# Holding the attention's operand splits behind the tanh and the gate of their slot, in a one-core attention and SwiGLU chain

## The chip, the cores and the metric

The kernel runs on one core of a Trainium2 chip. The metric is the device time of one launch in microseconds. Three runs of the kernel before gave 1437.30, 1439.62 and 1440.31 us; the median, 1439.62 us, is the time before.

## The reference, cut to what matters

All arrays are fp32; batch 8, 8 heads, 576 rows, head size 64, 32 packing rows per head.

```python
def sm_attn(qq, kk, vv):                     # softmax(scale * qq @ kk.T) @ vv
    ...
p_packed = sm_attn(p, k, v)                  # 32 rows per head
x = sm_attn(q, p_packed, p_packed)           # 576 rows per head
x = x.transpose(0, 2, 1, 3).reshape(4608, 512)
h = x @ w_in                                 # 512 -> 2048
x = (h * sigmoid(h)) @ w_out                 # 2048 -> 512
out = (((x @ w1) * (x @ w2)) @ w3) @ w_out2  # 512 -> 1024 -> 512
```

## The kernel before

Nearly every product is made from split operands: an fp32 array is turned into a high part in fp32r (a copy, on ScalarE, L82) and a low part, the rest (a subtraction, on VectorE or GpSimd, L91), and TensorE does three matmuls, high by high, low by high and high by low (`mm3`, L98 to L100). A **split** below is this pair of operations.

The long first stage makes x from the attention and takes it through `w_in`, SiLU and `w_out`. It never makes x itself: the packed rows of a head are multiplied into `w_in` once (`PackIn`, "pack w_in": matmuls ps_m, results ms stored to m_d), and the softmax weights `a` of the second attention go through that product. The stage is a list of 256 **slots** (`items`): a slot is a batch b, one of two halves f of 288 tokens, and one of 16 column blocks m. In each slot, in the order of the code:

- `fetch` (from L782) brings a block of the product (mr) and splits it into mq, the high part on VectorE (L86), the low part on GpSimd;
- `emit_h`: six matmuls ps_h<-a,mq;
- `emit_x2`: twelve matmuls ps_x<-gh,wo for the slot three before (`LAG` = 3);
- `emit_g`: the **tanh** sg on ScalarE (L841), the **gate** gg = (sg + 1) * ps_h on VectorE (L846), then gg's split, gh on ScalarE and gl on GpSimd. ps_h has two banks, so the matmuls of a slot wait for the gate of the slot two before;
- steps of three **streams**: "x", the attention units `Pack` (first attention of one batch and half of its heads) and `Spread` (second attention), "y", `PackIn`, and "z", decoding of later weights. `over(lo, hi, units)` and `pack_in` spread a unit's steps evenly over slots lo to hi, and `due` counts the steps due by a slot: n * (i + 1 - lo) / (hi - lo), rounded up. That is a **place**.

While a unit's steps run, `HOOKS` prepare the next unit's operands: `load_v`, `turn0` and `turn1` (k or q rows in kq, split into x: high part on ScalarE, low part on VectorE, `Rows.turn`), `prepare` (the packing rows pr, split into pb, same engines), `split_v0` and, in the first step of a `Pack`, `split_v(1)` (the values vr, split into v in two parts: ScalarE, GpSimd). `PackIn.load_w` loads a piece of `w_in` (wz) and splits it into wi (ScalarE, GpSimd); three are loaded ahead (`WI` = 3) before the first ps_m. Units of the first two batches work unsplit (`plain`), so the splits start with batch 2.

Slots that the prediction speaks of: the steps of `Spread(1, 0)` and `Spread(1, 1)` lie in slots 5 to 13, the last two of them in slots 11 and 12, and hang the splits for `Pack(2, 0)` on these (x in slots 11 and 12, pb and the first part of v in 12). `Pack(2, 0)` to `Pack(3, 1)` have 16 steps over slots 26 to 37: two steps are due in slot 26 (second part of v, then `turn0` for the next unit), the third in slot 27 (`turn1`, `prepare`), the fourth in slot 28. The `PackIn` of batches 2 and 3 starts in slot 44, the next ones in slots 102 and 166.

What is written is not the order of issue. The program is given to a scheduler at build time (last lines of `kernel`: `schedule_with_timeline_sim=True`), which plays it through with estimated times and sets each engine's own order; an engine then takes its instructions strictly in that order, waiting on semaphores. An operation whose data are there early may be put ahead of a tanh that was written long before it. `tc.issue_after(ins)`, used by `hold`, forbids that: what a block issues on the engine of `ins` is put behind `ins` in that engine's order. It adds no waiting for data. `behind["sg"]` and `behind["gg"]` are the latest tanh and gate that the code has written. The kernel before uses `hold` for the later weights' work only (`decode_late`, `prepare_second`), and similar blocks for the late half of `fetch` and for transfers.

Of the kernel before, what the change touches and what calls it, by code (L numbers as in the profile page):

```python
# [23 lines left out]
def attention_swiglu_chain(  # L24
# [54 lines left out]
    V, A, T, G, DMA = nc.vector, nc.scalar, nc.tensor, nc.gpsimd, nc.sync  # L79

    def act_copy(dst, src, mul=1.0):
        A.activation(out=dst, in_=src, func=ACTF.Copy, scale=mul)  # L82

    def split_hi(hi, src, on_vector=False):
        if on_vector:
            V.tensor_copy(out=hi, in_=src)  # L86
        else:
            act_copy(hi, src)

    def split_lo(lo, src, hi, eng=None):  # L90
        (eng or V).tensor_tensor(out=lo, in0=src, in1=hi.bitcast(F32), op=ALU.subtract)  # L91

    def split(hi, lo, src, on_vector=False, eng=None):
        split_hi(hi, src, on_vector)
        split_lo(lo, src, hi, eng)
# [8 lines left out]
    def hold(*names):  # L104

        stack = ExitStack()
        for x in names:
            stack.enter_context(tc.issue_after(behind[x]))
        return stack

    def move(out, in_, eng=DMA):

        out, in_ = (x.bitcast(F32) if x.dtype == F32R else x for x in (out, in_))
        with tc.issue_after(behind[eng]) if eng in behind else ExitStack():
            return eng.dma_start(out=out, in_=in_)  # L115
# [184 lines left out]
    class Rows:  # L300
# [25 lines left out]
        def turn(self, f):  # L326

            if f not in self.halves or self.lane.plain:
                return
            if f == self.halves[0]:  # L330
                self.xp = self.lane.parts([128, 2, S], "x")
            x = [t[:, :, f * HS:(f + 1) * HS] for t in self.xp]
            split(*x, self.rows[f])
            self.x[f] = [[t[:, e] for t in x] for e in range(2)]

        def turn0(self):
# [22 lines left out]
    class Pack(Rows):  # L359
# [22 lines left out]
        def prepare(self):  # L382
            if not self.lane.plain:
                self.pb = self.lane.parts([128, 2, 128], "pb")
                split(*self.pb, self.p)

        v_in_pieces = False

# [15 lines left out]
        def split_v(self, f):  # L404
            if self.lane.plain:
                return
            if f == 0:
                self.vp = self.lane.parts([128, 5, 4, 64], "v")
            r, cs = self.PARTS[f]
            hi, lo, src = (x[0:r, cs] for x in (*self.vp, self.v))  # L410
            split_hi(hi, src)
            split_lo(lo, src, hi, G)

        def split_v0(self):
            self.vp = [self.v]
# [81 lines left out]
    class PackIn:  # L497
# [14 lines left out]
        def load_w(self, i):  # L512
            if i < 4 * CD:
                g, c = divmod(i, CD)
                z = at.tile([128, 512], F32, tag="z", name="wz", bufs=NZ)
                move(out=z, in_=wi_d[g, 128 * c:128 * c + 128])
                t = at.tile([128, 2, 512], F32R, tag="wi", name="wi", bufs=WI)
                split_hi(t[:, 0], z)
                split_lo(t[:, 1], z, t[:, 0], G)
                self.w[i] = t  # L520

        def steps(self):
# [427 lines left out]
    def prepare_second():  # L950

        attn.close()
        with tc.tile_pool(name="dec2", bufs=1, side="right") as dp:
# [73 lines left out]
            for n in range(2 * KM2 + 2):  # L1027
                with hold("sg", "gg", "h"):
                    if n > 1:
                        product(n - 2)  # L1030
                    if n < 2 * KM2:
                        turn(n)
                for y in range(2):
                    with hold("sg", "gg"):
                        if used[0] < min(len(late) - KM2, KM2 + 3 + 3 * (n + y) // 2):
                            step()
                        some(2)
                    yield
# [362 lines left out]
```

## Time and profile before

| | |
|---|---|
| median of three runs | 1439.62 us |
| the profiled execution's own time | 1437.96 us |
| its span on the core | 1436.1 us |
| PE (TensorE matmul) busy | 1390.7 us, 97% |
| PEld (TensorE weight load) busy | 1308.4 us, 91% |
| DVE (VectorE) busy | 901.6 us, 63% |
| ACT (ScalarE) busy | 672.2 us, 47% |
| POOL (GpSimd) busy | 605.5 us, 42% |
| mean granted clock of TensorE | 0.992 |

Times inside the execution are microseconds from the start of the span. The 256 tanhs run from 52 us to about 855 us; from there on only the second half of the chain runs. A row of a timeline gives start, duration, engine, line, operation, what is written and read, shape and count, and in brackets how long the engine stood idle before it and what ended that. A granted clock of 1.00 is 2.4 GHz, of 0.50 is 1.2 GHz. PE is busy nearly all the time, so what matters are the few microseconds in which it stands idle or runs at the lower clock.

### The profile page before, as it was taken

How to read it: one execution, taken by the hardware profiler on the slowest of the kernel's cores; microseconds unless marked ns; L12 is line 12 of the kernel's file. 1: busy time of each engine (PE TensorE's matmuls, PEld its weight loads, DVE VectorE, ACT ScalarE, POOL GpSimd, SP SyncE). 2: the span in 40 equal slices, each digit the busy share in tenths (PEclk: the TensorE clock that was granted, in tenths of full speed). 3: DMA queues.
4: the chain of work that ended last, by engine and by line, in shares of the span. 5: the costliest groups of instructions: out<-in, count | busy, mean ns of one | idle time of the engine just before them, and what ended most of it. 6: DMA issues, size and time to landing. Idle time of an engine off the chain costs nothing.

```text
span 1436.1 us, 25890 instructions
## 1 busy us (share of the span) xinstructions
PE 1390.7 (97%) x9548; PEld 1308.4 (91%) x9548; DVE 901.6 (63%) x1687; ACT 672.2 (47%) x1474; POOL 605.5 (42%) x626
## 2 busy tenths in 40 slices
PE   7799899999999999999999999999999999999998
PEld 5578899899999999999998998999999999999998
DVE  5897756558766488666578855635454553645453
ACT  6866556655666555664556544323232231322221
POOL 2778755856779657687567534100000000000000
PEclk9999899999999999999999999999999999999999
DMA  8697544844568343563557667011010110101000
GB/s 319 198 308 253 163 150 142 265 152 146 170 184 249 123 155 121 170 190 116 178 162 252 204 228 298 23 38 46 15 60 1 60 29 31 59 2 60 1 30 30
DMA packets 135967, 193.07 MB, mean 134 GB/s; under 512 B 14496, under 2 KB 92576, under 8 KB 135328
## 3 DMA queue, kind: packets, MB, share of 16 engines
q1 hardware_dynamic: 125344, 178.82, 39.1%
q10 hardware_dynamic: 10496, 12.59, 2.5%
q8 instruction: 75, 1.23, 0.4%
q14 instruction: 52, 0.43, 0.1%
HBM read 132.38 MB, written 58.98 MB: 133 GB/s over the span
## 4 chain that ended last, share of the span: by engine, by line
PE 70%; DVE 9%; DMA 7%; issue 4%; POOL 4%; ACT 4%; SPq 2%; ACTq 0%; DVEq 0%; POOLq 0%
PE ps_ab L1236 24%; PE ps_x L100 6%; PE ps_x L98 6%; PE ps_x L99 6%; PE ps_o L98 5%; PE ps_o L99 5%; PE ps_o L100 5%; PE ps_h L98 3%; PE ps_h L100 3%; PE ps_h L99 3%; SPq L115 2%; DMA mr<-m_d 1%; DMA m_d<-ms 1%; POOL z L189 1%; DVE sbd L251 1%
## 5 line engine op out<-in xcount | busy, mean ns | idle before, releaser
L98 PE MATMUL ps_x<-gh,wo 128*128 128x288 f32 x1024 | 301.9, 298 | 2.7 <-ACT gh L82 1.2
L99 PE MATMUL ps_x<-gh,wo 128*128 128x288 f32 x1024 | 301.0, 296 | 0.0
L100 PE MATMUL ps_x<-gl,wo 128*128 128x288 f32 x1024 | 289.1, 297 | 1.9 <-POOL gl L91 1.6
L91 POOL TENSOR_TENSOR gl<-gg,gh 128x288 fp32r<-128x288 f32 x256 | 227.9, 893 | 101.5 <-ACT gh L82 82.5
L1236 PE MATMUL ps_ab<-xct,w 128*128 128x256 f32 x1728 | 223.0, 284 | 1.7 <-DVE r L1257 1.4
L1236 PEld LDWEIGHTS ps_ab<-xct,w 128*128 128x128 f32 x1728 | 215.6, 190 | 3.0 <-DVE r L1257 1.6
L98 PEld LDWEIGHTS ps_x<-gh,wo 128*128 128x128 f32 x1024 | 193.0, 189 | 6.1 <-DVE xs L883 2.0
L99 PEld LDWEIGHTS ps_x<-gh,wo 128*128 128x128 f32 x1024 | 193.2, 189 | 2.1 <-issue 1.2
L100 PEld LDWEIGHTS ps_x<-gl,wo 128*128 128x128 f32 x1024 | 188.1, 189 | 4.3 <-POOL gl L91 3.6
L82 ACT ACTIVATE gh<-gg 128x288 fp32r<-128x288 f32 x256 | 112.8, 443 | 165.8 <-DVE gg L846 158.2
L91 POOL TENSOR_TENSOR mq<-mr,mq 128x256 fp32r<-128x256 f32 x168 | 136.7, 814 | 109.0 <-DVE mq L86 54.4
L846 DVE SCALAR_TENSOR_TENSOR gg<-sg,ps_h 128x288 f32<-128x288 f32 x256 | 114.6, 448 | 107.3 <-ACT sg L841 55.3
L1236 PE MATMUL ps_ab<-xcb,w 128*128 128x256 f32 x1296 | 177.5, 283 | 0.7 <-ACT w L82 0.4
L98 PE MATMUL ps_h<-a,mq 128*128 128x288 f32 x512 | 155.9, 305 | 18.0 <-DVE gg L846 13.8
L1236 PEld LDWEIGHTS ps_ab<-xcb,w 128*128 128x128 f32 x1296 | 168.1, 189 | 5.6 <-ACT w L82 0.6
L1257 DVE TENSOR_TENSOR r<-p,ps_ab 128x512 f32<-128x512 f32 x72 | 49.2, 683 | 184.3 <-PE ps_ab L1236 184.1
L99 PE MATMUL ps_h<-a,mq 128*128 128x288 f32 x512 | 152.4, 298 | 0.0
L100 PE MATMUL ps_h<-a,mq 128*128 128x288 f32 x512 | 151.9, 297 | 0.0
L841 ACT ACTIVATE sg<-ps_h 128x288 f32<-128x288 f32 x256 | 103.4, 404 | 82.3 <-PE ps_h L100 48.6
L98 PEld LDWEIGHTS ps_h<-a,mq 128*128 128x128 f32 x512 | 96.7, 189 | 25.9 <-DVE gg L846 19.0
L82 ACT ACTIVATE p<-ps_ab 128x512 f32<-128x512 f32 x72 | 43.1, 598 | 146.2 <-PE ps_ab L1236 139.8
L100 PE MATMUL ps_o<-w,abh 128*128 128x512 f32 x280 | 109.5, 391 | 0.0
(172 smaller groups left out, 2645.3 us busy)
## 6 DMA issues: line engine op xcount, KB each, us to landing
mr<-m_d SPq DMA_DIRECT2D x144, 128.0 KB, 2.6
raw<-in_moe_w_dram SPq DMA_DIRECT2D x32, 512.0 KB, 4.4
wz<-wi_d SPq DMA_DIRECT2D x48, 256.0 KB, 3.8
m_d<-ms SPq DMA_DIRECT2D x96, 128.0 KB, 3.0
x_d<-xs SPq DMA_DIRECT2D x20, 576.0 KB, 3.4
raw<-in_moe_w_out_dram SPq DMA_DIRECT2D x22, 512.0 KB, 4.3
out_dram<-ob SPq DMA_DIRECT2D x36, 256.0 KB, 2.0
vr<-in_v_dram SPq DMA_DIRECT2D x14, 640.0 KB, 4.1
```

Of the source, the lines that this page charges most:

```text
L82: A.activation(out=dst, in_=src, func=ACTF.Copy, scale=mul)
L91: (eng or V).tensor_tensor(out=lo, in0=src, in1=hi.bitcast(F32), op=ALU.subtract)
L98: T.matmul(out=dst, lhsT=wh, rhs=xh, start=start, stop=False)
L99: T.matmul(out=dst, lhsT=wl, rhs=xh, start=False, stop=False)
L100: return T.matmul(out=dst, lhsT=wh, rhs=xl, start=False, stop=stop)
L115: return eng.dma_start(out=out, in_=in_)
L189: G.tensor_tensor(out=z, in0=z, in1=word(I32, 0), op=ALU.add)
L251: (act_copy if plain else V.tensor_copy)(dst[r, 0, :, r], src[r])
L841: ins = A.activation(out=sg, in_=ps, func=ACTF.Tanh, scale=0.5)
L846: ins = V.scalar_tensor_tensor(out=gg, in0=sg, scalar=1.0, in1=ps, op0=ALU.add, op1=ALU.mult)
L1236: T.matmul(out=bank[:, x], lhsT=w[:, wp], rhs=xt[:, kt, xp], start=first and (x, kt, n) == (0, 0, 0), stop=last and (x, kt, n) == (1, 1, 2 ...
L1257: V.tensor_tensor(out=dst, in0=p, in1=q, op=op)
```

## The change

Four places get a `hold`: the splits of x and pb go behind the latest tanh on ScalarE and behind the latest gate on VectorE; the splits of v and wi go behind the latest tanh on ScalarE (their low parts run on GpSimd, to which no hold applies, but they need the high part first). Nothing is added, removed or resized, and the slots at which the code writes these operations are the same.

```diff
@@ -330,7 +330,8 @@   (Rows.turn)
             x = [t[:, :, f * HS:(f + 1) * HS] for t in self.xp]
-            split(*x, self.rows[f])
+            with hold("sg", "gg"):
+                split(*x, self.rows[f])
             self.x[f] = [[t[:, e] for t in x] for e in range(2)]
@@ -382,7 +383,8 @@   (Pack.prepare)
                 self.pb = self.lane.parts([128, 2, 128], "pb")
-                split(*self.pb, self.p)
+                with hold("sg", "gg"):
+                    split(*self.pb, self.p)
@@ -408,8 +410,9 @@   (Pack.split_v)
             hi, lo, src = (x[0:r, cs] for x in (*self.vp, self.v))
-            split_hi(hi, src)
-            split_lo(lo, src, hi, G)
+            with hold("sg"):
+                split_hi(hi, src)
+                split_lo(lo, src, hi, G)
@@ -515,8 +518,9 @@   (PackIn.load_w)
                 t = at.tile([128, 2, 512], F32R, tag="wi", name="wi", bufs=WI)
-                split_hi(t[:, 0], z)
-                split_lo(t[:, 1], z, t[:, 0], G)
+                with hold("sg"):
+                    split_hi(t[:, 0], z)
+                    split_lo(t[:, 1], z, t[:, 0], G)
                 self.w[i] = t
```

## Rows read from the trace of the kernel before

**Rows 1.** PE's waits from 100 to 700 us: total, times, longest

```profile
PE ps_h L98 <- DVE gg L846: 9.3, 12, 2.7
PE ps_s L98 <- DVE mbd L492: 1.9, 4, 0.8
```

**Rows 2.** Timeline of ACT, 145 to 147 us: the x splits and a tanh

```profile
145.45 1.26 ACT L82 ACTIVATE x<-kq 128x576 fp32r<-128x576 f32 x2
...
146.91 0.41 ACT L841 ACTIVATE sg<-ps_h 128x288 f32<-128x288 f32 x1
```

**Rows 3.** The tanh's line from 0 to 146.9 us: count, shortest/median/longest ns, first and last start

```profile
L841 ACT ACTIVATE sg<-ps_h x27: 383/396/415, 52.4 to 142.4; 128x288 f32<-128x288 f32 x27
```

**Rows 4.** Timeline of DVE, 149 to 154 us

```profile
149.09 1.27 DVE L91 TENSOR_TENSOR x<-kq,x 128x576 fp32r<-128x576 f32 x1
150.29 1.49 DVE L91 TENSOR_TENSOR pb<-pr,pb 128x256 fp32r<-128x256 f32 x1
151.70 0.44 DVE L846 SCALAR_TENSOR_TENSOR gg<-sg,ps_h 128x288 f32<-128x288 f32 x1
...
153.46 0.45 DVE L846 SCALAR_TENSOR_TENSOR gg<-sg,ps_h 128x288 f32<-128x288 f32 x1
```

**Rows 5.** Timeline of PE, 150 to 170 us, two matmuls after idle time

```profile
152.20 0.40 PE L98 MATMUL ps_h<-a,mq 128*128 128x288 f32 x1 [1.32 <-DVE gg L846]
...
168.55 0.61 PE L98 MATMUL ps_h<-a,mq 128*128 128x288 f32 x1 [2.69 <-DVE gg L846]
```

**Rows 6.** Timeline of POOL, 153 to 169 us

```profile
153.91 2.58 POOL L91 TENSOR_TENSOR wi<-wz,wi 128x512 fp32r<-128x512 f32 x2
...
159.96 1.34 POOL L91 TENSOR_TENSOR wi<-wz,wi 128x512 fp32r<-128x512 f32 x1
...
164.17 3.07 POOL L91 TENSOR_TENSOR v<-vr,v 128x768 fp32r<-128x768 f32 x2
```

**Rows 7.** Timeline of DVE, 161 to 169 us: the casts ahead of a gate

```profile
162.96 4.33 DVE L251 CAST sbd<-pkT 32x64 fp32r<-32x64 f32 x4
```

**Rows 8.** Instructions on tile sbd, whole span: count, shortest/median/longest ns, first and last start

```profile
L251 DVE CAST sbd<-pkT x48: 175/306/2066, 163.0 to 588.4; 32x64 fp32r<-32x64 f32 x48
```

**Rows 9.** Stretches: length, busy time of each engine, granted clock, DMA share, GB/s

```profile
82.00:95.00 13.00, 13.00 (x84) 11.47 (x83) 11.54 (x18) 9.62 (x22) 10.85 (x11) 1.00 0.92 283
95.00:111.00 16.00, 12.90 (x78) 10.31 (x78) 15.76 (x24) 8.94 (x18) 10.03 (x11) 1.00 0.93 306
141.00:153.00 12.00, 8.78 (x59) 7.46 (x58) 11.97 (x18) 8.15 (x20) 11.30 (x10) 1.00 0.57 172
153.00:164.00 11.00, 10.82 (x71) 10.59 (x71) 5.50 (x16) 7.35 (x18) 10.78 (x12) 0.84 0.73 209
164.00:176.00 12.00, 9.31 (x50) 9.08 (x49) 10.17 (x22) 3.61 (x9) 7.04 (x9) 0.72 0.24 73
200.00:215.00 15.00, 15.00 (x118) 15.00 (x117) 8.96 (x28) 7.33 (x18) 10.25 (x12) 1.00 0.56 177
```

**Rows 10.** Timeline of DVE, 83 to 104 us

```profile
83.78 1.54 DVE L91 TENSOR_TENSOR pb<-pr,pb 128x256 fp32r<-128x256 f32 x1
...
102.75 0.75 DVE L91 TENSOR_TENSOR x<-kq,x 128x576 fp32r<-128x576 f32 x1
103.42 0.44 DVE L846 SCALAR_TENSOR_TENSOR gg<-sg,ps_h 128x288 f32<-128x288 f32 x1
```

**Rows 11.** Instructions on tile pb, whole span: columns as in rows 8

```profile
L91 DVE TENSOR_TENSOR pb<-pr,pb x12: 408/412/1536, 83.8 to 549.6; 128x256 fp32r<-128x256 f32 x12
```

**Rows 12.** Timeline of POOL, 98 to 106 us: its longest idle time there

```profile
104.14 0.74 POOL L91 TENSOR_TENSOR mq<-mr,mq 128x256 fp32r<-128x256 f32 x1 [2.60 <-DVE mq L86]
```

**Rows 13.** Instructions on tile wi, whole span: the first matmul of each product

```profile
L98 PE MATMUL ps_m<-wi,mbd x48: 388/393/500, 236.6 to 647.0; 128*128 128x512 f32 x48
```

**Rows 14.** Timeline of DVE, 277 to 283 us

```profile
279.99 1.18 DVE L86 CAST mq<-mr 128x256 fp32r<-128x256 f32 x1 [3.33 <-DMA mr<-m_d]
```

**Rows 15.** Timeline of PE, 277 to 283 us

```profile
281.59 0.40 PE L98 MATMUL ps_h<-a,mq 128*128 128x288 f32 x1 [1.04 <-DVE gg L846]
```

## The prediction

> **What bounds the kernel now.** I read the stretches first, then PE's waits, then the timelines around the longest waits. From 200 us on PE is busy without a break for long stretches [rows 9], so only its idle time and its time at the lower clock can be won. In the 600 us in which the moved splits lie, PE waits 9.3 us in 12 places for a gate and 1.9 us in 4 for the blocks mbd [rows 1]. A gate is late when VectorE has other work queued ahead of it: from 95 to 111 us VectorE works 15.76 of 16 us, from 141 to 153 us 11.97 of 12, and there PE stands idle 16 - 12.90 = 3.1 and 12 - 8.78 = 3.2 us [rows 9]. After the second of these the granted clock falls: 0.84 over 11 us is 11 * 0.16 / 0.5 = 3.5 us at 1.2 GHz, and 0.72 over 12 us is 6.7 us; at half the rate these cost half their length, 1.75 and 3.35 us [rows 9].
>
> **What the change moves.** A hold only matters where a split now stands ahead of the tanh or gate of its slot. I paired the n-th split of a kind on ScalarE with the n-th that the plan of places issues, and counted tanhs. Of 132 splits 39 stand ahead: 12 of x, 8 of pb, 10 of v, 9 of wi. Most x and pb are early by one to nine slots, the second parts of v by 19 to 32, the first three wi of each of the three products by 15 to 45. The other 93 are behind already, some by five slots, and stay. An example: 27 tanhs have run by 146.9 us [rows 3], so the one at 146.91 is slot 27's, and the two x splits just before it [rows 2] are those of slots 26 and 27. Consumers are far: the first three wi run at about 152 us and their first matmul at 236.6 [rows 6, 13].
>
> **Slots 26 to 28.** On VectorE gate 27 starts at 151.70, behind x of slot 27 and pb, 1.27 and 1.49 us [rows 4]. Held, these follow it: it starts at 149.09 and ends at 149.5. They then end by 152.3 at the same lengths, before gate 28's 153.46, so gate 28 need not be later. PE's idle of 1.32 us before 152.20 [rows 5] goes: **-1.3 us** (0 to -1.3).
>
> **The clock after it.** With 3.2 - 1.3 = 1.9 us of idle in 12, the stretch is below the 3.1 in 16 from 95 to 111 us that kept the full clock [rows 9]. I count the first fall as gone: **-1.75 us**. The second I leave; the bounds are 0 and -1.75 - 3.35 = -5.1.
>
> **Slots 28 to 33.** The three wi of slot 44 take 2.58 + 1.34 = 3.9 us of GpSimd ahead of two v splits that run from 164.17, 3.07 us [rows 6]. Beside these v the four sbd casts take 4.33 us [rows 7], against a median of 0.31 each, 1.2 for four [rows 8], and they stand ahead of the gate for which PE waits 2.69 us [rows 5]. With the wi gone to slot 44 the v can run up to 3.9 us sooner, mostly before the casts. The v are in their own slots and stay in the order. I take **-2.0 us** of the wait; bounds 0 and -2.69.
>
> The Trainium skill (SBUF — State Buffer, Who interferes with whom) says that VectorE and GpSimd share one port pair under an exclusive lock, and that the loser is blocked for the whole instruction. These rows agree, a cast's longest being 2.07 us against 0.31. By that rule the casts would lose all of 4.33 - 1.2 = 3.1 us and the wait would go whole; the sum below would be 0.7 us lower. The same rule speaks against every GpSimd half that lands beside a VectorE chain in its new slot.
>
> **Slots 11 to 13.** Here the change brings work in. pb and both v now run around 83 us, in a stretch in which PE never idles (13.00 of 13), so nothing is won there [rows 9, 10]. pb and the first v go to slot 12, the stretch from 95 us whose VectorE is full. x of slot 12 stands ahead of gate 12 (102.75, then 103.42) [rows 10]; behind it, it delays gate 13 instead, which cancels. pb is new work ahead of gate 13: 0.41 us undisturbed, 1.54 beside GpSimd [rows 11, 10]. The v on GpSimd has a gap of 2.60 us [rows 12], and using it puts GpSimd beside pb, so I take the price beside it: **+1.5 us** (0.4 to 1.5).
>
> **v's second part in slot 26.** GpSimd is full from 141 to 153 us, 11.30 of 12 [rows 9]; half of a pair of v parts is 3.07 / 2 = 1.5 us [rows 6]. It pushes gl, which has three slots until its matmuls. **+0.4 us** (0 to 1.5), near nothing since PE's long waits are for gates and not for gl [rows 1].
>
> **Slots 66 to 68.** The wi of slot 102 run from 278 us. A cast of mq takes 1.18 us there and PE idles 1.04 us behind the gate after it; but the cast itself waited 3.33 us for a transfer, which stays [rows 14, 15]. **-0.7 us** (0 to -1.04).
>
> **Slots 85, 86, 149, 150.** v of these slots runs two or three slots early and ahead of the copies pk, whose chain pkT, sbd, mbd ends in the waits for mbd, 1.9 us in all [rows 1]. Held, pk goes first, but v then falls beside the same chain. **-0.8 us** (-1.9 to +1.4).
>
> **The rest** costs nothing as long as its cover holds. From 200 to 215 us PE is busy 15.00 of 15 us and GpSimd 10.25, which leaves room for the 3.9 us of wi [rows 9]; the first ps_m is 30 us away [rows 13]. The groups of slots 59, 72, 102, 122, 136 and 166 are alike; if GpSimd lacks the room, gl is late next. Bounds 0 to +1.5. No transfer is held, and none is issued earlier: a held split frees its source tile later, but the tiles are reloaded a unit later.
>
> **Sum.** -1.3 - 1.75 - 2.0 + 1.5 + 0.4 - 0.7 - 0.8 = -4.65 us. The profiled execution took 1437.96 us, 1.66 below the median of 1439.62, so 1433.3 there and **1435.0 us** as a median. The best ends give -1.3 - 5.1 - 2.69 + 0.4 - 1.04 - 1.9 = -11.6, the worst +1.5 + 1.5 + 1.4 + 1.5 = +5.9.
>
> **Rivals.**
>
> *Given back.* VectorE has the same work, and where it is full a split that is passed by one gate delays the next. For it: VectorE's 11.97 of 12 us, with decoding work queued there too [rows 9]. Against it: the 5.50 of 11 us right behind, where held work could go [rows 9]. Then the gate's 1.3 us, both falls of the clock and the waits of slots 85 and 149 stay, GpSimd's relief remains: -2.0 + 1.5 + 0.4 - 0.7 = -0.8, 1438.8 us, no change that a measurement shows.
>
> *Little is moved.* The scheduler's estimated times are not the chip's, and it may fill the freed places on VectorE with other work written earlier (decoding). Then the gates are as late as now and the time is about 1439.6. For it: decoding shares VectorE where it is full [rows 9]. Against it: gate 27 has no decoding between the splits and itself [rows 4].
>
> *Slower.* VectorE's chain in slots 11 to 15 becomes the bound. x of slot 12 and pb come between gates 12 and 13 with v on GpSimd beside them, and run at 1.27 and 1.54 instead of 0.75 and 0.41 us [rows 4, 10, 11]: +0.5 for x, +1.5 for pb as the sum has it. PE's idle of 3.1 us in that stretch becomes over 5, and the granted clock falls there as it does after 153 us, +1.75 for the shorter fall. With slots 26 to 33 given back (v's second part takes the room of the wi there, +1.5), this is 0.5 + 1.5 + 1.75 + 1.5 = +5.25 less 1.5 from the later slots (0.7 + 0.8), +3.75: 1443.4 us. It decides when PE idles over 5 us between 95 and 111 us.
>
> **How the numbers follow.** A measurement of this kernel tells about 0.2%, 2.9 us, from no change. My forecast has 0.47, all of it counted as faster; given back 0.22 and little moved 0.11, both within 0.2%; slower 0.20. The range reaches from the forecast with the second fall and the whole of the long wait gone too (-4.65 - 3.35 - 0.7 = -8.7, 1430.9, a little lower for the other bounds: 1430) up to the slower case, 1443.5. Cases of one sign do not hold most of it; the forecast's own range is 1430 to 1437.
>
> **What would show it.** Right: gate 27 directly behind its tanh, the wait of 2.69 us under 1 us, a granted clock near 1.00 from 153 to 164 us, three wi behind the 45th tanh. PE's waits for gates from 100 to 700 us near 5 us. Wrong: the same waits a slot or two later, a granted clock below 1.00 between 95 and 115 us, or new waits of PE for gl or for ps_m's operands.

## The result and the profile after

The kernel after takes **1451.43 us** (four runs, 1449.99 to 1453.49), the kernel before 1438.97 beside it: ratio 1.0092, 95% interval 1.0077 to 1.0106. It is slower by about 12.5 us, where 1435.0 was forecast. The hold does what it says: of the 132 splits none stands ahead of its slot's tanh or gate any more (39 did). So the rival "little is moved" is out; the work moved, and it cost.

The page's busy times after (engine, busy us, share of the span, instructions):

```profile
span 1451.3 us, 25880 instructions
PE 1395.6 (96%) x9548; PEld 1311.6 (90%) x9548; DVE 917.8 (63%) x1687; ACT 672.4 (46%) x1474; POOL 618.0 (43%) x626
```

VectorE is busy 16.2 us and GpSimd 12.5 us longer than before, with the same instructions: they stand in each other's way more. The tile x shows it, VectorE's 48 low parts of x before and after (count, shortest/median/longest ns, first and last start):

```profile
L91 DVE TENSOR_TENSOR x<-kq,x x48: 709/749/1869, 101.3 to 665.7; 128x576 fp32r<-128x576 f32 x48
L91 DVE TENSOR_TENSOR x<-kq,x x48: 740/912/3911, 105.9 to 689.8; 128x576 fp32r<-128x576 f32 x48
```

PE's waits of the kernel after from 100 to 700 us, to be set against [rows 1]:

```profile
PE ps_h L98 <- DVE gg L850: 14.5, 14, 4.3
PE ps_s L98 <- DVE mbd L495: 5.8, 4, 2.0
```

Gates cost 5.2 us more (9.3 before), mbd 3.9 more (1.9 before). The stretches of after, columns as in [rows 9]; the last line is that of 215 to 230 us before:

```profile
95.00:111.00 16.00, 13.28 (x86) 11.35 (x85) 15.96 (x25) 10.61 (x22) 10.55 (x10) 1.00 1.01 330
141.00:153.00 12.00, 9.69 (x67) 8.76 (x66) 12.00 (x16) 9.73 (x22) 11.37 (x10) 1.00 0.65 195
153.00:164.00 11.00, 6.32 (x39) 5.83 (x38) 10.08 (x15) 4.15 (x13) 10.07 (x11) 0.79 0.45 125
164.00:176.00 12.00, 12.00 (x87) 12.00 (x86) 6.31 (x12) 4.25 (x11) 7.13 (x8) 0.91 0.44 132
200.00:215.00 15.00, 15.00 (x118) 15.00 (x117) 8.11 (x24) 10.44 (x26) 10.54 (x12) 1.00 0.64 192
215.00:230.00 15.00, 13.02 (x86) 12.64 (x85) 13.18 (x32) 6.37 (x17) 9.67 (x11) 0.89 0.33 99
...
215.00:230.00 15.00, 15.00 (x118) 15.00 (x118) 8.92 (x24) 9.89 (x25) 8.01 (x10) 1.00 0.36 120
```

PE's long idle time has moved from the stretch of 164 to 176 us to the one of 153 to 164 us, and a fall of the clock with an idle gap stands at 215 to 230 us, where PE was busy 15.00 of 15 us before. Three places show what the moved work meets.

**Slot 12, near 103 us.** Timelines of VectorE, GpSimd and PE:

```profile
102.91 2.09 DVE L91 TENSOR_TENSOR pb<-pr,pb 128x256 fp32r<-128x256 f32 x1
...
102.79 1.92 POOL L91 TENSOR_TENSOR v<-vr,v 128x768 fp32r<-128x768 f32 x1
...
109.30 0.40 PE L98 MATMUL ps_h<-a,mq 128*128 128x288 f32 x1 [2.55 <-DVE gg L850]
```

The held pb and the held v start within 0.12 us of each other. pb takes 2.09 us (0.41 undisturbed [rows 11]), and the gates behind it come late.

**Slots 26 to 29, near 155 us.** The same three engines:

```profile
155.15 3.91 DVE L91 TENSOR_TENSOR x<-kq,x 128x576 fp32r<-128x576 f32 x1
158.99 1.48 DVE L91 TENSOR_TENSOR pb<-pr,pb 128x256 fp32r<-128x256 f32 x1
...
161.24 0.45 DVE L850 SCALAR_TENSOR_TENSOR gg<-sg,ps_h 128x288 f32<-128x288 f32 x1
...
154.98 1.35 POOL L91 TENSOR_TENSOR v<-vr,v 96x512 fp32r<-96x512 f32 x1
156.29 0.73 POOL L91 TENSOR_TENSOR mq<-mr,mq 128x256 fp32r<-128x256 f32 x1
156.99 0.78 POOL L91 TENSOR_TENSOR gl<-gg,gh 128x288 fp32r<-128x288 f32 x1
157.73 0.71 POOL L91 TENSOR_TENSOR mq<-mr,mq 128x256 fp32r<-128x256 f32 x1
...
161.75 0.61 PE L98 MATMUL ps_h<-a,mq 128*128 128x288 f32 x1 [4.34 <-DVE gg L850]
```

The x split of slot 27 starts just after v's second part and takes 3.91 us. It ends at 159.06, after GpSimd has run these four instructions one behind the other (to 158.44). pb follows, and the gate comes at 161.24. PE is idle for 4.34 us, and the granted clock is 0.79 from 153 to 164 us.

**Slot 48, near 220 us.** The held wi of slot 44 run on GpSimd ahead of a pair of v splits, with one gl between. These v had been behind their tanh already:

```profile
210.93 2.54 POOL L91 TENSOR_TENSOR wi<-wz,wi 128x512 fp32r<-128x512 f32 x2
...
214.19 3.09 POOL L91 TENSOR_TENSOR v<-vr,v 128x768 fp32r<-128x768 f32 x2
...
215.68 2.63 DVE L251 CAST sbd<-pkT 32x64 fp32r<-32x64 f32 x4
...
219.53 1.99 DVE L253 TENSOR_TENSOR sbd<-pkT,sbd 32x64 fp32r<-32x64 f32 x4
221.55 0.22 DVE L493 CAST mbd<-ps_pk 64x64 fp32r<-64x64 f32 x1
...
223.15 0.38 PE L98 MATMUL ps_s<-x,pb 128*128 128x288 f32 x1 [1.98 <-DVE mbd L495]
```

The chain sbd, mbd is stretched by v and by two mq behind it, and PE waits 1.98 us. A granted clock of 0.89 over these 15 us is 15 * 0.11 / 0.5 = 3.3 us at 1.2 GHz, 1.65 us more. A wait of 2.01 us of the same kind stands at 394.5 us (slot 100).

To compare kernels stage by stage I use **PE's lost time**: from each matmul's start to the next one's, less the median of that for matmuls with the same operands by name, summed over the slots between two tanhs. It takes in idle time and the lower clock alike. In us, worked out from each kernel's trace:

```
slots                to 12   12-26   26-44   44-66   66-86  86-104 104-140  140 on     all
before                22.1     5.0    11.4     0.9     3.4     2.1     0.8    17.3    63.0
after                 25.3     8.2     9.0     7.3     1.8     6.8     0.1    19.6    77.9
e1_x_only             25.0     3.5    12.7     0.6     3.3     2.5     0.9    15.4    64.0
e2_pb_only            24.8     3.2    13.0     1.5     1.6     3.1     0.0    15.8    62.8
e3_v_only             24.9     8.1    13.1     4.9     1.0     6.4    -0.2    16.2    74.4
e4_wi_only            26.1     4.7     5.9     3.3     3.6     3.0     3.9    15.8    66.2
e5_v_second           25.3     6.2     9.9     0.7     2.6     8.8    -0.1    18.7    72.2
e6_v_first            22.8     6.7    11.2     3.1     1.8     8.1     0.0    16.1    69.8
e7_v_late             24.1     5.0     9.9     3.0     0.3     4.8    -0.2    18.8    65.6
e8_v_moved            25.7     7.6     9.1     4.0     0.9     4.8     0.9    18.3    71.3
e9_v_two              24.9     7.9    11.9     1.0     2.6     2.6     0.9    15.6    67.4
e10_lo_held           24.6     5.2    15.6     3.1     0.4     5.2     0.7    19.5    74.3
e11_no_v              24.4     3.5     7.0     5.2     2.2     2.7     2.0    17.9    64.8
e12_rest_v_late       24.2     3.5     7.3     6.9     1.9     6.8     0.7    16.0    67.3
e13_early             24.0     7.8     9.2     5.1     3.2     2.2     0.9    16.4    68.9
e14_late              22.1     5.0    10.8     4.6     0.4     6.8     0.3    17.2    67.4
e15_wi_spread         25.5     4.7     6.0     1.3     3.8     2.3     0.3    16.2    60.2
e16_no_wi             24.6     6.9    14.6     1.3     1.1     6.7     0.5    16.2    71.7
e17_wi_first          23.6     4.7     6.2     4.3     2.6     2.5     4.2    15.1    63.2
e18_wi_spread_all     26.3     4.7     6.0     1.5     5.6     5.6     0.8    18.4    68.9
```

After loses 14.9 us more than before in the profiled executions: 3.2 in slots 12 to 26, 6.4 in slots 44 to 66, 4.7 in slots 86 to 104, 3.2 ahead of slot 12 (where e15, which is faster than before, loses 3.4 more too) and some at the end; it gains 2.4 in slots 26 to 44 and 1.6 in slots 66 to 86. So the stall near 155 us adds nothing to the loss against before: it takes the place of the long wait and the falls of the clock that stood there [rows 5, 9], and eats up part of a relief (with wi alone held, e4, these slots lose 5.9).

### The profile page after: what moved, and what is told of

Its sections match the earlier page's. It is cut to its first block, busy times and chain, and to the rows that moved or that the text cites. A ratio compares the mean times of both kernels' runs of the same rounds, so it can differ in the third digit from the quotient of the medians.

```text
span 1451.3 us, 25880 instructions
## 1 busy us (share of the span) xinstructions
PE 1395.6 (96%) x9548; PEld 1311.6 (90%) x9548; DVE 917.8 (63%) x1687; ACT 672.4 (46%) x1474; POOL 618.0 (43%) x626
## 4 chain that ended last, share of the span: by engine, by line
PE 71%; DVE 10%; DMA 6%; ACT 5%; issue 4%; POOL 2%; SPq 1%; ACTq 0%; DVEq 0%; POOLq 0%
PE ps_ab L1240 24%; PE ps_x L100 6%; PE ps_x L98 6%; PE ps_x L99 6%; PE ps_o L98 5%; PE ps_o L99 5%; PE ps_o L100 5%; PE ps_h L98 3%; PE ps_h L100 3%; PE ps_h L99 3%; DMA z<-late_d 2%; SPq L115 1%; DMA mr<-m_d 1%; DVE gg L850 1%; DMA m_d<-ms 1%
## 5 line engine op out<-in xcount | busy, mean ns | idle before, releaser
L100 PE MATMUL ps_x<-gl,wo 128*128 128x288 f32 x1024 | 293.0, 297 | 1.1 <-POOL gl L91 0.9
L91 POOL TENSOR_TENSOR gl<-gg,gh 128x288 fp32r<-128x288 f32 x256 | 232.1, 908 | 112.6 <-ACT gh L82 88.6
```

Source lines behind the costliest of these rows:

```text
L100: return T.matmul(out=dst, lhsT=wh, rhs=xl, start=False, stop=stop)
```

## The experiments

All ratios are against the kernel before of the same group of runs; medians in us.

```
run                  held                                          median   before   ratio [95%]
e1_x_only            x                                             1439.69  1438.31  1.0008 [0.9996, 1.0020]
e2_pb_only           pb                                            1438.97  1438.31  1.0002 [0.9992, 1.0011]
e3_v_only            v                                             1449.07  1438.31  1.0066 [1.0045, 1.0086]
e4_wi_only           wi                                            1439.42  1438.31  1.0012 [1.0003, 1.0021]
e5_v_second          v's second parts                              1442.8   1437.7   1.0044 [1.0029, 1.0060]
e6_v_first           v's first parts                               1445.7   1437.7   1.0061 [1.0044, 1.0078]
e7_v_late            v of batches 4 to 7                           1438.71  1437.7   1.0005 [0.9993, 1.0017]
e8_v_moved           v, both parts in the slot of the first        1447.1   1437.7   1.0067 [1.0052, 1.0082]
e9_v_two             v of Pack(2, 0): two splits                   1443.91  1437.6   1.0047 [1.0030, 1.0064]
e10_lo_held          GpSimd's half of v                            1450.26  1437.6   1.0088 [1.0073, 1.0103]
e11_no_v             the change without v                          1443.39  1437.6   1.0036 [1.0024, 1.0048]
e12_rest_v_late      the change without e9's two splits            1442.58  1437.6   1.0030 [1.0018, 1.0042]
e13_early            the change in slots 0 to 44                   1444.09  1438.08  1.0037 [1.0023, 1.0052]
e14_late             the change from slot 45 on                    1442.96  1438.08  1.0032 [1.0022, 1.0042]
e15_wi_spread        first product's wi, spread over three slots   1435.42  1438.08  0.9975 [0.9963, 0.9986]
e16_no_wi            the change without wi                         1446.74  1438.08  1.0057 [1.0042, 1.0071]
e17_wi_first         first product's wi, all in slot 44            1438.74  1438.34  1.0007 [0.9996, 1.0017]
e18_wi_spread_all    all three products' wi, spread                1441.96  1438.34  1.0027 [1.0016, 1.0039]
```

**One hold at a time.** Each of the four kernels is the kernel before with one of the change's four holds, for example

```diff
-            split_hi(hi, src)
-            split_lo(lo, src, hi, G)
+            with hold("sg"):
+                split_hi(hi, src)
+                split_lo(lo, src, hi, G)
```

for v.

> Only the splits of x are held (12 of 48 move, by one to nine slots). Theory 'place' (a held split costs what it delays in its new slot, above all where VectorE's chain is full and GpSimd works beside it; the parts add up to the change's +12.5 us): +1 to +3 us, from slots 12 and 27. Theory 'redrawn' (the held splits cost little themselves, the scheduler's new order of all the other work does): a difference of up to 5 us either way that has nothing to do with the stretches where x moves, and the four parts don't add up. Theory 'late' (consumers wait for the split): waits of PE at ps_s for x, over 2 us.

> Only the splits of pb are held (8 of 12 move, by one to 22 slots). 'Place': +1 to +2 us, at slots 12 to 14. 'Redrawn': anything within 5 us either way, in other stretches. 'Late': waits of PE at ps_s.

> Only the splits of v are held (10 of 24 move, the second parts by 18 to 32 slots). 'Place': the largest part, +4 to +8 us, since the GpSimd half (1.3 to 1.9 us) blocks VectorE beside it in slots 12, 26, 72, 85, 86, 136. 'Redrawn': within 5 us either way, waits elsewhere. 'Late': waits of PE at ps_o.

> Only the splits of wi are held (9 of 48 move, by 15 to 45 slots). 'Place': they leave full stretches (150, 280 us) for slots 44, 102 and 166, where GpSimd has room: -1 to -4 us, by the relief that the prediction counted (2.0 for the long wait before 168.5 us, 0.7 near 281 us, more if the clock holds). 'Redrawn': within 5 us either way, elsewhere. 'Late': waits of PE at ps_m.

v alone brings most of the loss, x and pb nothing that can be measured, wi a little, where 'place' had a gain for it. But wi alone does relieve: slots 26 to 44 fall from 11.4 to 5.9 us of lost time; it is given back in slots 44 to 66 (+2.4) and 104 to 140 (+3.1). The relief does not come about as the prediction had it, with v ahead of the casts. In e4, GpSimd, VectorE and PE, to be set against [rows 5, 6, 7]:

```profile
164.42 3.09 POOL L91 TENSOR_TENSOR v<-vr,v 128x768 fp32r<-128x768 f32 x2
...
164.76 3.79 DVE L251 CAST sbd<-pkT 32x64 fp32r<-32x64 f32 x4
...
170.81 0.40 PE L98 MATMUL ps_h<-a,mq 128*128 128x288 f32 x1 [1.04 <-DVE gg L847]
```

v still runs beside the casts, which take 3.79 us (4.33 before). PE waits 1.04 us there instead of 2.69, and from 141 to 176 us the granted clock stays at 1.00, though PE idles 0.60, 0.26, 0.96 and 1.32 us on its way to 155.91 us, just as before on its way to 152.20 (0.60, 0.25, 0.97 and 1.32).

With v alone the stall near 155 us is there again, with another victim. VectorE and GpSimd of e3:

```profile
158.49 3.34 DVE L449 TENSOR_TENSOR rs<-sm 128x1 f32<-128x1 f32 x1
...
162.13 0.45 DVE L847 SCALAR_TENSOR_TENSOR gg<-sg,ps_h 128x288 f32<-128x288 f32 x1
...
158.38 1.32 POOL L91 TENSOR_TENSOR v<-vr,v 96x512 fp32r<-96x512 f32 x1
159.66 0.72 POOL L91 TENSOR_TENSOR mq<-mr,mq 128x256 fp32r<-128x256 f32 x1
160.34 0.79 POOL L91 TENSOR_TENSOR gl<-gg,gh 128x288 fp32r<-128x288 f32 x1
161.09 0.72 POOL L91 TENSOR_TENSOR mq<-mr,mq 128x256 fp32r<-128x256 f32 x1
```

An addition of one element per partition, 150 ns at the median of its 16, takes 3.34 us: it starts just behind v's start and ends when GpSimd's four instructions are through (161.09 + 0.72 = 161.81). So the length of the victim does not bound its loss. Why it is let in then and not earlier stays open: GpSimd works without a gap before v and behind these four, too.

**Which v.** The condition of the hold is `f == 1` (second parts), `f == 0` (first parts) or `self.b > 3`; the fourth holds all and writes the second part right behind the first:

```diff
+            with hold("sg") if f == 1 else ExitStack():
...
     def split_v0(self):
...
             self.split_v(0)
+            self.split_v(1)
```

> Only the second parts of v are held (slot 26 instead of about 7, 72 instead of 51, 136 instead of 104, and 86, 150). Theory 'GpSimd beside a full VectorE' (the GpSimd half of v, now in slots 12 and 26, fills GpSimd's last gaps, and VectorE instructions beside it are shut out for several microseconds): slot 26 carries the longest block, so +3 to +6 us. Theory 'redrawn' (the new order of the other work costs): no relation, within 5 us either way. Theory 'late': PE waits at ps_o <- v.

> Only the first parts of v are held (slot 12 instead of about 7, 59 instead of 51, 122 instead of 104, and 85, 149). 'GpSimd beside a full VectorE': slot 12 carries +2 to +3 us, slot 59 another +1 to +3; with the other half the two should add up to about +9.5 us. 'Redrawn': no relation, the two do not add up.

> v is held for batches 4 to 7 only (slots 59, 72, 85, 86, 122, 136, 149, 150), not for the first group (slots 12 and 26). 'GpSimd beside a full VectorE': the first 150 to 170 us stay as before, and what is left is +2 to +5 us, from 250 to 400 us. 'Redrawn': as many matmuls are reordered as with the first group held, so about the whole +9.5 us.

> v is held as in the change, but the second part is written in the slot of the first (12, 59, 85, 122, 149 instead of 26, 72, 86, 136, 150). 'GpSimd beside a full VectorE': the block of slot 26 goes and the long instructions on VectorE from 150 to 160 us with it: +2 to +6 us instead of +9.5. 'Redrawn': about +9.5 us as before. 'Late': better than +9.5 us only if PE's waits at ps_o <- v go away, and there are none to go.

Either part alone costs (1.0044 and 1.0061, more together than both at once, 1.0066), and writing the second part elsewhere does not mend it, as 'redrawn' had it: in e8 slots 26 to 44 lose 4.0 us less than in e3, but slots 12 to 26 still lose 7.6, and the time is 9.4 us longer than before. v of the later batches alone costs nothing that can be measured (in e7 slots 86 to 104 lose 2.7 us more, slots 66 to 86 3.1 less), so the price of v alone hangs on batches 2 and 3. Since the parts don't add up, I cut by place next.

**Two splits, and which engine's half.** e9 holds only v of Pack(2, 0), the splits of slots 12 and 26; e12 is the change with just these two left free. e10 leaves ScalarE's half of v where it was and holds GpSimd's half behind the latest gl on GpSimd:

```diff
+            with hold("sg") if self.b == 2 and self.hg == 0 else ExitStack():
...
             split_hi(hi, src)
+            with hold("gl"):
+                split_lo(lo, src, hi, G)
```

The first line is e9's (e12 has the opposite condition), the last two are e10's.

> Held are only the two v splits of the first unit of batch 2, 264 KB in all: the first part in slot 12 (ran at 82.6 us) and the second in slot 26 (83.3 us). All other holds are left out. Theory 'place': the loss of PE's time between slots 12 and 26 (5.0 us before, 8.1 with all v held) and little elsewhere: +3 to +5 us. Theory 'propagated' (the two splits also shift the order of all the work behind them, and the stretch of slots 86 to 104, where PE lost 2.1 us before and 6.4 to 8.8 with v held, goes wrong without any hold in it): +7 to +9 us with 3 us or more of it in slots 86 to 104. Theory 'spread' (every held v costs a little): +1 to +2 us.

> ScalarE's half of each v split stays where it was before, early; only GpSimd's half is held, behind the last gl of its slot on GpSimd. 'GpSimd' theory (its half of v beside VectorE's chain is the cost): +5 to +9.5 us, as with the whole split held. 'ScalarE' theory (its 0.62 and 0.84 us ahead of gh and the next tanh): 0 to +2 us.

> The change without its hold on v: x, pb and wi are held. If the parts add up: 0.5 + 0.3 + 1.7 = +2.5 us or less. If the holds only cost together (any theory of interplay): +5 us or more.

> The whole change except for the two v splits of the first unit of batch 2, which are not held. 'Place' and 'propagated': the +12.5 us shrink to +1 to +4 us. 'Spread': +10 us or more.

Two splits out of 24 bring 1.0047 by themselves, half of the loss, and letting them go early takes the change from 1.0092 to 1.0030. PE's long waits in e9 from 95 to 170 us:

```profile
108.45 0.61 PE L98 MATMUL ps_h<-a,mq 128*128 128x288 f32 x1 [3.33 <-DVE gg L847]
...
156.85 0.40 PE L98 MATMUL ps_h<-a,mq 128*128 128x288 f32 x1 [1.78 <-DVE gg L847]
161.80 0.61 PE L98 MATMUL ps_h<-a,mq 128*128 128x288 f32 x1 [3.56 <-DVE gg L847]
```

The wait near 108 us is the new one. Those of 1.78 and 3.56 us take the place of two waits of the kernel before (1.32 and 2.69 us [rows 5]), and slots 26 to 44 lose 11.9 us, 11.4 before; slots 12 to 26 lose 7.9, 5.0 before. The change says the same: without these two holds (e12) slots 12 to 26 lose 4.7 us less (3.5 for 8.2) and slots 26 to 44 only 1.7 less (7.3 for 9.0). Behind slot 44 e9 loses nothing more than before (1.0, 2.6 and 2.6 us against 0.9, 3.4 and 2.1). In e10 ScalarE's half is unheld and the time is as long (1.0088), so a loss of this size needs no late half on ScalarE. But it stands elsewhere: slots 12 to 26 lose 5.2 us, as before, and slots 26 to 44 lose 15.6. That GpSimd's half alone makes the loss of slot 12 is not shown. The change without any hold on v still loses 1.0036, more than x, pb and wi one by one (0.0022 together). So a second cause was open, in slots 44 to 104.

**Early or late, and wi.** In e13 and e14 all four holds apply only to splits written up to slot 44, or only from slot 45 on; e16 is the change without wi's hold; e15 holds nothing but the first product's three wi, each behind an earlier tanh (slots 37, 39, 41) instead of all behind slot 44's:

```diff
+    def hold_some(*names):
+        return hold(*names) if behind["slot"] < 45 else ExitStack()
...
+                with tc.issue_after(tanhs[2 * i - 8]) if i < WI and self.bs[0] == 2 else ExitStack():
                     split_hi(t[:, 0], z)
                     split_lo(t[:, 1], z, t[:, 0], G)
```

The first function is e13's (`> 44` in e14), the rest e15's; `tanhs` lists the tanhs in the order written.

> All four holds, but only for splits that are written in slots 0 to 44 (batches 2 and 3's units, and the first three wi). If the later losses of the whole change (PE's lost time in slots 44 to 66 and 86 to 104, 7.3 and 6.8 us against 0.9 and 2.1) follow from what the early holds did to the order of issue: about 1448 to 1451 us, both stretches again at 6 or more. If each loss has its hold in its own place: the early part alone, slots 86 to 104 at 2 to 3 us and 1444 to 1447 us.

> All four holds, but only for splits that are written from slot 45 on. If the later losses follow from the early holds: no change that can be measured, 1437 to 1440 us, slots 86 to 104 at 2 to 3 us. If each loss has its hold in its own place: slots 86 to 104 at 6 to 7 us, and 1441 to 1444 us.

> Only the first product's first three wi are held, behind the tanhs of slots 37, 39 and 41 rather than all behind that of slot 44. If GpSimd's relief in slots 26 to 33 is worth what the run with wi alone showed (slots 26 to 44 fell from 11.4 to 5.9 us of lost time) and the loss behind it came from three wi in one slot: slots 26 to 44 at 6 to 8 us, slots 44 to 66 near 1 us, 1433 to 1436 us, faster than both kernels. If the new order of the program gives it back wherever the wi stand: 1437 to 1440 us.

> The change without the hold on wi. If the three wi in slot 44 push the two v splits that run behind them onto the casts sbd and mbd, for which PE waits 2.1 us in slot 48: that wait and the fall of the clock behind it are gone, slots 44 to 66 at 3 to 5 us instead of 7.3, and 1446 to 1449 us. If wi's hold only relieves (slots 26 to 44): slots 26 to 44 back at 12 to 13 us and 1451 to 1454 us.

Early and late holds cost 0.37 and 0.32%, 0.69 of the 0.92 together, and slots 86 to 104 lose 6.8 us with the late holds and 2.2 with the early ones. So that loss comes from holds in its own neighbourhood, not from the early ones by way of a new order. The table says which: the ten kernels that hold v splits of batches 4 to 7 lose 4.8 to 8.8 us there, the ten that do not lose 2.1 to 3.1, apart from e18 with 5.6, which holds wi there. PE's waits of e14 from 200 to 420 us, with the same wait of 2.0 us in slot 100 as after:

```profile
PE ps_s L98 <- DVE mbd L498: 3.2, 2, 2.0
PE ps_m L98 <- ACT ms L82: 1.8, 3, 1.1
PE ps_m L98 <- DVE s L578: 1.0, 1, 1.0
```

Slots 44 to 66 lose in both (5.1 and 4.6): early it is the wait of slot 48, late waits at ps_m. Which late holds, next to v's, make the single wait of slot 100 is not settled. It is in the runs that hold the later v together with x and pb (after, e12, e14, e16), and neither in e3 (v alone) nor in e11 (no v). The v pair there is not moved by its own hold, since it was behind its tanh before; what differs is the order of a gate, an mq and the sbd casts around it.

Without wi's hold the wait in slot 48 is gone. PE's waits from 180 to 300 us, of e16:

```profile
PE ps_s L98 <- ACT ms L82: 0.9, 1, 0.9
PE ps_m L98 <- ACT ms L82: 0.4, 2, 0.2
```

and the longest of the kernel after:

```profile
PE ps_s L98 <- DVE mbd L495: 2.0, 1, 2.0
```

Slots 44 to 66 lose 1.3 us instead of 7.3, but slots 26 to 44 lose 14.6 instead of 9.0: wi's relief and wi's burst, seen in one run.

**A version that beats both.** e15 keeps the relief without the burst: 0.9975, about 2.7 us faster than before. GpSimd and the stretches of e15, which answer to [rows 6, 9]:

```profile
181.94 1.29 POOL L91 TENSOR_TENSOR wi<-wz,wi 128x512 fp32r<-128x512 f32 x1
...
188.80 1.29 POOL L91 TENSOR_TENSOR wi<-wz,wi 128x512 fp32r<-128x512 f32 x1
...
196.29 1.44 POOL L91 TENSOR_TENSOR wi<-wz,wi 128x512 fp32r<-128x512 f32 x1 [1.46 <-ACT wi L82]
```

```profile
153.00:164.00 11.00, 9.55 (x71) 9.16 (x72) 7.28 (x17) 7.51 (x20) 10.48 (x13) 1.00 0.63 182
164.00:176.00 12.00, 10.45 (x77) 10.01 (x76) 11.32 (x26) 5.07 (x15) 6.89 (x8) 1.00 0.36 105
176.00:200.00 24.00, 24.00 (x186) 23.93 (x185) 15.67 (x43) 14.03 (x38) 14.35 (x15) 1.00 0.51 165
```

The clock stays at 1.00 where it was 0.84 and 0.72, and the three wi fit into gaps of GpSimd between 181 and 198 us, where PE is never idle. e15 differs from e4 in two things, the spreading and that only the first product is held. Two more runs change one each:

```diff
+                with hold("sg") if self.bs[0] == 2 else ExitStack():
+                with tc.issue_after(tanhs[2 * i - 8]) if i < WI else ExitStack():
```

The first line is e17's, the second e18's.

> Only wi is held, behind the tanh of slot 44 as in the change, but for the first product alone. If spreading the three wi over three slots is what kept the relief: slots 44 to 66 lose 3 us as with wi alone (1.3 when spread) and the time is 1437 to 1439 us. If the loss came from the holds of the second and third product (slots 104 to 140 lost 3.9 us with wi alone, 0.8 before): as fast as the spread version, 1434.5 to 1436.5 us.

> As the spread version (wi behind the tanhs eight, six and four slots before the first place of its product's steps plus one), for all three products. If three wi in one slot were the cost of the later products' holds: slots 104 to 140 near 1 us, and as fast as the spread version or up to 2 us faster, 1433 to 1436 us. If any later start of those wi costs, wherever they stand: slots 104 to 140 at 3 us or more, 1437 to 1440 us.

Held in one slot (e17) the first product's wi bring no gain that can be measured: slots 44 to 66 lose 4.3 us. Slots 104 to 140 lose 4.2 as with all three products held, though e17 holds nothing there: in slot 113 PE waits 2.46 us for ms. That part does follow from the new order of issue. Spread for all products (e18), slots 104 to 140 are clean, but PE now waits near 382 and 577 us, 2.3 and 2.4 us, and the kernel is slower, which neither expectation had. So both matter: spreading, and leaving the later products alone.

## Why the prediction was wrong, step by step

Forecast -4.65 us, measured +12.5, beyond the range (1430 to 1443.5). The mechanism was wrong, not only a size. The sum asked whether a moved split fits into the idle time of its new slot and how far its consumers are. It left out, or priced too low, what GpSimd's half does there to VectorE's chain ahead of a gate or of mbd, directly or by pushing other splits onto it. The step that failed most is "the rest", counted as 0, where slots 44 to 66 lose 6.4 us; next come slots 85 and 86, then slot 12.

- **Slots 26 to 28, -1.3 us: failed.** Gate 27 was to follow its tanh directly. Its tanh starts at 151.10, the gate at 153.72 behind the x split of slot 26, and gate 28 only at 161.24. The step took the held splits "at the same lengths", and the same change put v's second part beside them: x takes 3.91 us instead of 1.27 [rows 4].
- **The clock, -1.75 us: right in size, not for the reason given.** From 153 to 176 us before was 3.5 + 6.7 us at 1.2 GHz; after it is 11 * 0.21 / 0.5 + 12 * 0.09 / 0.5 = 6.8 us, 1.7 us of time less. But PE idles longer, 2.31 + 4.68 = 7.0 us from 141 to 176 us where it idled 3.22 + 0.18 + 2.69 = 6.1. And the 1.3 us of idle time that the step took out do not decide: e4 has them still and keeps 1.00.
- **Slots 28 to 33, -2.0 us: near in size, by luck.** With wi alone (e4) the wait behind the casts falls by 1.65 us, and slots 26 to 44 lose 5.5 us less, most of it the clock; with wi spread (e15) that is kept. But v was to run mostly before the casts, and runs beside them as before (e4), in the kernel after too (v from 172.24, the casts 3.57 us from 172.25). What shortens the wait is not shown.
- **Slots 11 to 13, +1.5 us: mis-sized.** pb did land beside v as priced, at 2.09 rather than 1.54 us. The step stopped there; x ran beside gl and mq too (1.06 us), and PE idles 2.55 us. Slots 12 to 26 lose 3.2 us more than before, and 4.7 more than with the two v splits left early (e12). The gap of GpSimd that I filled with v [rows 12] was not free: VectorE worked in it.
- **v's second part in slot 26, +0.4 us: wrong in kind, and too low.** I priced it as a delay of gl, since no long wait of PE was for gl. Its price is what it does to VectorE beside it: x or a 128x1 addition loses up to 3.2 us (3.91 - 0.74, 3.34 - 0.15). Left early together with slot 12's part (e12), slots 26 to 44 lose 1.7 us less, above my bound of 1.5.
- **Slots 66 to 68, -0.7 us: not gained by the move of wi.** The kernel after has waits for a gate of 1.13 us at 285.23 and of 1.35 us at 300.19. Slots 66 to 86 do lose 1.6 us less, but they lose still less without wi's hold (1.1 in e16), and with wi alone 3.6 (3.4 before).
- **Slots 85 and 86, 149 and 150, -0.8 us: wrong sign.** Waits for mbd grew by 3.9 us over the whole stretch, one of 2.0 us in slot 100, beyond my worst end of +1.4. Slots 86 to 104 lose 4.7 us more, and they do so wherever the later v are held.
- **The rest, 0 (to +1.5): failed most.** Room was counted as GpSimd's idle time from 200 to 215 us. There was room (10.54 us busy after), but three wi in one slot pushed the v pair behind them onto the sbd and mbd chain: 1.98 us of wait and 1.65 us of clock in slot 48. Slots 44 to 66 lose 7.3 us, 1.3 without wi's hold (e16). I had asked whether the moved work fits, not who stands behind it and what that then meets.

Of the rivals, "slower" had the sign and the mechanism (held work beside v in a full stretch of VectorE), and slots 12 to 26 do lose 3.2 us more. But from 95 to 111 us PE idles 16 - 13.28 = 2.7 us, not over 5, the clock stays at 1.00 there, and the larger losses stand in slots 44 to 66 and 86 to 104, where it counted a gain of 1.5. The rule of the Trainium skill (SBUF — State Buffer, Who interferes with whom) that I weighed for slots 28 to 33 speaks of the loser being blocked for the whole instruction; taken alone it would make x lose one v, 1.35 us. The trace shows more: x and rs<-sm ended only when four instructions of GpSimd were through. The trace before had shown it too: its longest cast of sbd [rows 8] runs from 523.62 to 525.69 us, over a v and the gl behind it (524.84 to 525.64), so "these rows agree" was half the reading.

## What to carry to other kernels

Before a hold moves an operation that has a half on GpSimd, price that half by what VectorE runs beside it in its new place and by what it pushes onto others behind it, not by whether its own consumers are far. To relieve a crowded stretch, hold its movable work behind staggered points of the next quiet stretch, not all behind one slot, and run it: here three splits held so were the whole gain (e15), and the same for the later products made the kernel slower (e18). The parts of this change did not add up (x, pb and wi 1.0008, 1.0002 and 1.0012 singly, 1.0036 together), and a hold can cost where it holds nothing (e17), so each combination has to be run.

## What the runs showed of the hardware that was not expected

A VectorE operation with both inputs in SBUF stayed shut out over several back-to-back instructions of GpSimd: 3.91 us for x (0.74 at the shortest), 3.34 us for a 128x1 addition (150 ns at the median). The same sight is in e9 (rs<-sm, 3.34 us) and e13 (x, 3.91 us), each time from just behind the start of v's second part. The gates beside the same work are never stretched; in the kernel after (columns as above, all 256):

```profile
L850 DVE SCALAR_TENSOR_TENSOR gg<-sg,ps_h x256: 393/453/457, 54.5 to 875.8; 128x288 f32<-128x288 f32 x128
```

They read one input from SBUF and one from PSUM. The same page of the Trainium skill, SBUF — State Buffer, section Who interferes with whom, says that an instruction with at most one SBUF input, outside the two-port modes, does not contend with GpSimd; a longest of 457 ns against a median of 453 agrees. So a gate is late here because of what stands ahead of it.
